# Room by rank of expert resized in a routed mixture of experts, with float32 first layers for seven ranks and wide pairs for two others

## The chip, the cores and the metric

The kernel runs on one core of a Trainium2 chip. The core has five engines that run side by side, each through its own queue in order: TensorE (PE in the profile, its weight loads shown apart as PEld), VectorE (DVE), ScalarE (ACT), GpSimd (POOL) and SyncE (SP), which mainly issues transfers. Transfers run on 16 DMA engines. Matrix products are written to PSUM, a memory of eight banks for each partition; everything else lies in SBUF. The metric is the device time of one execution in microseconds (us).

## The reference, cut to what matters

Two stages follow each other. The first is a recurrent attention with gates over 768 steps for 4 batches and 8 heads; its output, 3072 tokens of 320 numbers, is the input of the second. The change touches the second stage alone:

```python
g_logits = x @ w_group                       # 3072 tokens, 4 groups
g_idx = np.argmax(g_logits, axis=1)          # and its softmax weight g_w
...
e_idx = np.argmax(xg @ w_expert[g], axis=1)  # 4 experts a group, weight e_w
...
h = np.maximum(xg[mask_e] @ w1[g, e], 0.0)   # 320 -> 1024
ye = h @ w2[g, e]                            # 1024 -> 320
out[tok_idx] = (g_w * e_w)[:, None] * ye
```

Each token goes to one of 16 experts, so the number of tokens of an expert is known only on the chip.

## The kernel before, in words

**Routing.** While attention runs, each chunk of 128 steps is routed, and the tokens' numbers are written to a table in device memory (`itab`), a stretch for each expert. The experts are then ranked by their counts, the fullest first. What is compiled is a row of 16 ranks, rank r with fixed room for `CAPS[r]` tokens; which expert stands at a rank is read from a register when its weights are loaded. Rank 0's expert is picked early and done in two pieces, `EARLY` (256) tokens before the routing has ended and `LATE` after it, keys (0, 0) and (0, 1). Tokens beyond the room of their rank are done 128 at a time by a loop at the end (`For_i` at L1062 and what follows), which runs as often as the counts ask.

**An expert.** `load_x` gathers its tokens in blocks of up to 128 rows (GpSimd, L578). `turn_tasks` turns each block with three transposes on TensorE (tile `tpm`) into `xhl`. `expert` then runs a first layer into the tile `psh` (three banks), a Relu into `hh`, and a second layer into `po` (two banks); the rows of `po` are scaled and scattered (L582) to their places in the output.

To keep float32 accuracy at the rate of a single pass, operands are split into a high and a low part (type float32r): `w1h`, `w1l`, `w2h`, `w2l` by `split_tasks` (ScalarE copies, VectorE subtracts, L638 and L640), tokens by `turn_tasks` (L682, L683), and `hh` by `relu` (ScalarE L697, VectorE L700). A first layer has one of three forms:

- Regular (L743): eight matmuls for each of the 8 slices f of 128 hidden units, 64 in all, with the expert's W tokens as moving columns. Two slices share a bank where W is at most 256.
- Wide pairs (`NARROW`, L722 to L728): high and low tokens stand side by side as 2W moving columns; three matmuls of 2W and two of W for each slice, 40 in all, each slice in a bank of its own. ScalarE copies one half out of PSUM and VectorE adds the other, then comes the Relu.
- Float32 (`FULL`, L711): three matmuls of type float32 for each slice, 24 in all, on the unsplit weights `w1s` and unsplit tokens. Nothing of w1 is split for such an expert, and `w1s` stays in use until its first layer ends. The rows of the third part of `xhl` that hold no token are cleared by GpSimd (L677).

The second layer has for each block of tokens 24 matmuls (L764 to L766) with the hidden units as stationary operand and 320 columns of w2 moving. A last block of at most 64 rows (`mp`) takes 16 instead (L769, L770, L772): its high and low hidden units stand side by side in `hh`, as one stationary operand of twice the columns, and the two halves of `po` are added afterwards (L778 to L780).

**Order.** Within the expert stage a scheduler lays out each engine's queue when the kernel is built. `hh` has one buffer; the split weights have two sets, used by ranks of even and odd number; `w1s` and `w2s`, the weights as loaded, have two buffers each. Rank r+2's weights and tokens are asked for at the head of rank r's turn in the loop (SyncE, L596 and L611), but for a `FULL` rank r the load of w1 for rank r+2 is put after r's first layer, since it needs r's buffer. Keys in `RETIRE` let GpSimd wait after their last scatter until its transfers are through (a drain, L786).

Of the kernel before, what the change touches and what calls it, by code (L numbers as in the profile page):

```python
# [7 lines left out]
F32 = mybir.dt.float32  # L8
F32R = mybir.dt.float32r
# [9 lines left out]
P = 128  # L19
# [5 lines left out]
NE = 16  # L25
F = 1024
NF = F // P
# [10 lines left out]

NEARLY, NPICK, EARLY, LATE = 1, 2, 256, 128
CAPS = [EARLY + LATE, 352, 320, 288, 256, 256, 256, 256, 192, 192, 192, 192, 160, 160, 160, 128]


NARROW = ((0, 1), (11, 0), (12, 0))

RETIRE = ((2, 0), (5, 0), (8, 0), (11, 0), (13, 0), (14, 0))


FULL = (13, 14, 15)  # L50


def bc(ap, shape):
# [4 lines left out]
def lstm_moe(ctx: ExitStack, tc: tile.TileContext, gates, qkT, nat, og, wcat, w1, w2, cst, out):  # L58
    nc = tc.nc
    enter = ctx.enter_context  # L60
    mm = nc.tensor.matmul
# [545 lines left out]
    def load_ix(r, q=None):  # L607
        nb = len(blocks(CAPS[r]))
        ixs[r] = mxp.tile([P, 3], I32, name="ix", bufs=5)
# [17 lines left out]
    pools = {}  # L627
# [3 lines left out]
    def split_tasks(r, now=True):  # L631
# [27 lines left out]

        first = [] if r in FULL else [lambda: w1part(0), lambda: w1part(1), wrest]  # L660
        return first + [lambda k=k: w2part(k) for k in range(4)]

    def turn_tasks(key, W, xg, banks=None):
        t = {}

        def one(i, m):
            if i == 0:
                pool = pools["xhl"][len(xhls) % len(pools["xhl"])]
                sh, dt = ([P, 3, W], F32) if key[0] in FULL else ([P, 3, 2, W], F32R)
                t["x"] = xhls[key] = pool.tile(sh, dt, name="xhl", bufs=1)  # L670
# [16 lines left out]
    def expert(key, W, ws, xg, idx, between=(), then=None, last=None):  # L687
        xhl = xhls[key]
        w1h, w1l, wsk, w2h, w2l = (ws.get(n) for n in ("w1h", "w1l", "wsk", "w2h", "w2l"))

        nf = W // P * P if 0 < W % P <= 64 else W
        mp = W - nf
        hh = pools["hp"].tile([P, NF, 2 * W], F32R, name="hh")

        def relu(f, per, src):
            hr = hh[:, f:f + per, 0:W]
            act = nc.scalar.activation(hr, src, AF.Relu)  # L697
            for dst, t in ((slice(W + mp, 2 * W), slice(0, nf)), (slice(W, W + mp), slice(nf, W))):
                if t.start < t.stop:
                    nc.vector.scalar_tensor_tensor(hh[:, f:f + per, dst], src[:, :, t], 0.0, hr.bitcast(F32)[:, :, t],  # L700
                                                   op0=ALU.max, op1=ALU.subtract)
            return act

        if key[0] in FULL:
            w1s = w1st[key[0]]
            for f in range(0, NF, 2):
                ps = pools["ps_h"].tile([P, 512], F32, name="psh")
                for g in range(2):
                    for k in range(3):
                        s = slice(k * F + (f + g) * P, k * F + (f + g + 1) * P)  # L710
                        ins = mm(ps[:, g * W:(g + 1) * W], w1s[:, s], xhl[:, k, :], start=(k == 0), stop=(k == 2))  # L711
                relu(f, 2, ps[:, 0:2 * W].rearrange("p (q w) -> p q w", q=2))
                do(between, 1)
        elif key in NARROW:
            xw, xh = [xhl[:, k].rearrange("p a w -> p (a w)") for k in range(3)], [xhl[:, k, 0, :] for k in range(2)]
            for f in range(0, NF, 2):
                hs = pools["hp"].tile([P, 2, W], F32, name="hs", bufs=2)
                for g in range(2):
                    ps = pools["ps_h"].tile([P, 512], F32, name="psh")
                    s0 = slice((f + g) * P, (f + g + 1) * P)  # L720
                    s1 = slice(F + (f + g) * P, F + (f + g + 1) * P)
                    mm(ps[:, 0:2 * W], w1h[:, s0], xw[0], start=True, stop=False)  # L722
                    mm(ps[:, 0:W], w1l[:, s0], xh[0], start=False, stop=False)
                    mm(ps[:, 0:W], w1l[:, s1], xh[1], start=False, stop=False)
                    mm(ps[:, 0:2 * W], w1h[:, s1], xw[1], start=False, stop=False)
                    ins = mm(ps[:, 0:2 * W], wsk[:, s0], xw[2], start=False, stop=True)
                    nc.scalar.copy(hs[:, g, :], ps[:, W:2 * W])
                    nc.vector.tensor_tensor(hs[:, g, :], hs[:, g, :], ps[:, 0:W], op=ALU.add)  # L728
                act = relu(f, 2, hs)
                if key[0] == 0:  # L730
                    do(between, 1)
        else:
            per = 2 if W <= 256 else 1
            for f in range(0, NF, per):
                ps = pools["ps_h"].tile([P, 512], F32, name="psh")
                for g in range(per):
                    s0 = slice((f + g) * P, (f + g + 1) * P)
                    s1 = slice(F + (f + g) * P, F + (f + g + 1) * P)
                    xh, xl = [xhl[:, k, 0, :] for k in range(3)], [xhl[:, k, 1, :] for k in range(3)]
                    todo = [(w1h, s0, xh[0]), (w1h, s0, xl[0]), (w1h, s1, xh[1]), (w1h, s1, xl[1]), (wsk, s0, xh[2]),  # L740
                            (wsk, s0, xl[2]), (w1l, s0, xh[0]), (w1l, s1, xh[1])]
                    for n, (w, s, x) in enumerate(todo):
                        ins = mm(ps[:, g * W:(g + 1) * W], w[:, s], x, start=(n == 0), stop=(n == len(todo) - 1))  # L743
                relu(f, per, ps[:, 0:per * W].rearrange("p (q w) -> p q w", q=per))
                if per == 2 or f % 2:
                    do(between, 1)
        if then:
            with tc.issue_after(ins.ins):
                do(then)
        if key in NARROW:  # L750
            with tc.issue_after(act.ins):
                do(between)
        for i, m in enumerate(blocks(W)):
            t = slice(i * P, i * P + m)
            tl = slice(W + mp + i * P, W + mp + i * P + m)
            po = pools["ps_o"].tile([P, DM], F32, name="po")
            for f in range(NF):
                s = slice(f * DM, (f + 1) * DM)
                st0, sp0 = f == 0, f == NF - 1
                if last and f == NF // 2 and i == len(blocks(W)) - 1:  # L760
                    with tc.issue_after(ins.ins):
                        do(last)
                if m > 64:
                    mm(po[0:m], hh[:, f, t], w2h[:, s], start=st0, stop=False)  # L764
                    mm(po[0:m], hh[:, f, t], w2l[:, s], start=False, stop=False)  # L765
                    ins = mm(po[0:m], hh[:, f, tl], w2h[:, s], start=False, stop=sp0)  # L766
                else:
                    if not st0:
                        mm(po[0:m], hh[:, f, t], w2l[:, s], start=False, stop=False)  # L769
                    mm(po[0:2 * m], hh[:, f, nf:nf + 2 * m], w2h[:, s], start=st0, stop=sp0)  # L770
                    if st0:
                        mm(po[0:m], hh[:, f, t], w2l[:, s], start=False, stop=False)  # L772
            y = pools["hp"].tile([P, DM], F32, name="y", bufs=3)
            comb = xg[i][0:m, 3 * P:3 * P + 1]
            if m > 64:
                nc.scalar.activation(y[0:m], po[0:m], AF.Copy, scale=comb)  # L776
            else:
                nc.scalar.copy(y[0:m], po[m:2 * m])  # L778
                nc.vector.tensor_tensor(y[0:m], y[0:m], po[0:m], op=ALU.add)
                nc.vector.tensor_scalar(y[0:m], y[0:m], comb, None, op0=ALU.mult)  # L780
            done = scatter(y[0:m], idx(i, m))
            no_order("out", done)
        if key in RETIRE:

            with tc.issue_after(done.ins):
                nc.gpsimd.drain()  # L786
# [241 lines left out]
    for r in range(NEARLY):  # L1028
        xgs[r, 1] = load_x(LATE, late_ix[r])
    xgs[1] = load_x(CAPS[1], ix_of(1))  # L1030
    load_w1(2, nc.gpsimd)
# [4 lines left out]
    with tc.issue_after(rt["last"].ins):  # L1036
        do(split, 3)
    expert((0, 1), LATE, wsp_[0], xgs[0, 1], late_ix[0], split, turn_tasks((1, 0), CAPS[1], xgs[1]))
    xgs[2] = load_x(CAPS[2], ix_of(2))
    for r in range(NEARLY, NE):  # L1040
        if r + 2 < NE:
# [4 lines left out]
            load_w2(r + 2, nc.gpsimd if r < 2 else None)  # L1046
            xgs[r + 2] = load_x(CAPS[r + 2], ix_of(r + 2))
        if r + 1 < NE:
            split = split_tasks(r + 1)
            if r + 1 not in FULL:  # L1050
                do(split, 3)
            then = turn_tasks((r + 1, 0), CAPS[r + 1], xgs[r + 1])
        else:
# [6 lines left out]
    hp = pools["hp"]  # L1060
    nv = nc.values_load(total[0:1, 0:1], min_val=0, max_val=NBLK + NE)
    with tc.For_i(0, nv, 1):  # L1062
# [36 lines left out]
        for f in range(NF):  # L1099
            ps = pools["ps_h"].tile([P, 512], F32, name="psh")  # L1100
            for k in range(3):
                kk = min(P, DM - k * P)
                mm(ps[:, 0:P], w1s[0:kk, k * F + f * P:k * F + (f + 1) * P], xT[0:kk, k, :], start=(k == 0),
                   stop=(k == 2))
            nc.vector.tensor_scalar(h[:, f, :], ps[:, 0:P], 0.0, None, op0=ALU.max)
        po = pools["ps_o"].tile([P, DM], F32, name="po")
        for f in range(NF):
            mm(po, h[:, f, :], w2s[:, f * DM:(f + 1) * DM], start=(f == 0), stop=(f == NF - 1))
        y = hp.tile([P, DM], F32, name="y", bufs=3)
# [69 lines left out]
```

## Time and profile before

| | us |
|---|---|
| median of three runs | 432.39 |
| lowest, highest | 429.99, 433.73 |
| the profiled execution | 433.8 |
| span of the profiled execution, first to last instruction | 432.2 |

The span falls into attention and routing (to about 177 us), rank 0 (to about 205 us), ranks 1 to 15 (to about 426 us) and a tail. Lines of the profile give an engine's busy time, and after a bar what its idle time waited for. A row of a view by stretches gives the stretch, its length, the busy time and number of instructions of TensorE, its weight loads, VectorE, ScalarE and GpSimd, then the granted clock, the share of the DMA engines and GB/s. An instruction counts in a stretch that it overlaps, so a number of instructions can be two or three above those that begin there. A float32 matmul appears as two entries. A row in order of time gives the start, the length, the line, and in brackets how long the engine was idle before it and what released it.

### The profile page before, as it was taken

To read this page: it belongs to the slowest core of one execution; us is meant where nothing else is said; L and a number is where in the kernel's file an instruction comes from. 1 tells how busy PE (TensorE), PEld (TensorE's weight loads), DVE (VectorE), ACT (ScalarE), POOL (GpSimd) and SP (SyncE) were. 2 spreads that over 40 slices of the span, in tenths; PEclk is the share of its full clock that TensorE was granted. 3 is DMA by queue.
4 is the path that set the end of the run, shared out by engine and by line. 5 is a ranking of instruction groups with operands and counts; after the bars stand their busy time and mean duration, and the time that the engine had idled before them with its cause. 6 is when DMAs were issued, how large, how long until landed. Compare 5 with 4: busy or idle time off the path is not lost.

```text
span 432.2 us, 10108 instructions
## 1 busy us (share of the span) xinstructions
PE 406.0 (94%) x3775; PEld 382.5 (89%) x3775; DVE 286.0 (66%) x714; ACT 230.8 (53%) x551; POOL 173.3 (40%) x220
## 2 busy tenths in 40 slices
PE   7879999999998893999999999999999999999994
PEld 4768999898888883799999999999999999999994
DVE  5595677768796963776747585575675877867420
ACT  5654454646566511527637474575656575765421
POOL 2335476666756335154432416213413432322210
PEclk9978899999998987599999999999999999999999
DMA  7974669995999942088975545586559666544300
GB/s 208 286 222 134 191 87 209 264 254 107 248 244 265 224 149 65 3 265 229 424 275 191 200 161 214 170 288 242 211 212 321 211 226 235 186 156 148 153 16 11
DMA packets 29495, 85.39 MB, mean 198 GB/s; under 512 B 12242, under 2 KB 16155, under 8 KB 25861
## 3 DMA queue, kind: packets, MB, share of 16 engines
q1 hardware_dynamic: 24068, 67.63, 54.0%
q0 software_dynamic: 5152, 16.75, 11.2%
q8 instruction: 30, 0.49, 0.5%
q10 hardware_dynamic: 224, 0.35, 0.4%
q14 instruction: 21, 0.16, 0.2%
HBM read 74.95 MB, written 10.62 MB: 198 GB/s over the span
## 4 chain that ended last, share of the span: by engine, by line
PE 71%; issue 11%; DVE 9%; DMA 4%; POOL 2%; POOLq 1%; ACT 1%; DVEq 0%
PE psh L743 21%; PE av L276 6%; PE po L764 6%; PE po L765 6%; PE po L766 6%; PE sp L204 3%; PE it L229 3%; PE tpm L306 3%; DMA sig<-in_og_dram 3%; PE aw L177 2%; PE po L770 2%; PE it L248 2%; PE po L769 2%; PE psh L711 2%; PE tp L306 1%
## 5 line engine op out<-in xcount | busy, mean ns | idle before, releaser
L187 ACT ACTIVATE ab<-aw,bcol 128x128 f32<-128x128 f32 x192 | 54.7, 371 | 53.3 <-PE aw L177 52.9
L578 POOL DMA_INDIRECT xg<-x_d,ix x34 | 40.4, 1189 | 81.5 <-DMA ix<-itab 47.4
L582 POOL DMA_INDIRECT out_dram<-y,ix x34 | 39.8, 1170 | 73.4 <-ACT y L776 58.9
L764 PE MATMUL po<-w2h,hh 128*128 128x320 f32 (+1 forms) x208 | 65.7, 316 | 0.0
L765 PE MATMUL po<-w2l,hh 128*128 128x320 f32 (+1 forms) x208 | 64.2, 309 | 0.0
L766 PE MATMUL po<-w2h,hh 128*128 128x320 f32 (+1 forms) x208 | 64.2, 309 | 0.0
L640 DVE TENSOR_TENSOR w2l<-w2s,w2h 128x640 fp32r<-128x640 f32 x64 | 50.2, 818 | 20.1 <-ACT w2h L638 20.1
L743 PE MATMUL psh<-xhl,w1h 128*128 128x256 f32 (+4 forms) x352 | 59.5, 290 | 0.9 <-DVE xhl L683 0.5
L276 PE MATMUL av<-nt,pt 128*128 128x128 f32 x384 | 52.9, 295 | 0.2 <-DVE pt L209 0.2
L743 PEld LDWEIGHTS psh<-xhl,w1h 128*128 128x128 f32 x352 | 50.3, 192 | 1.5 <-DVE xhl L683 0.8
L276 PEld LDWEIGHTS av<-nt,pt 128*128 128x128 f32 x384 | 50.4, 210 | 1.0 <-DVE pt L209 0.4
L700 DVE SCALAR_TENSOR_TENSOR hh<-psh,hh 128x256 fp32r<-128x256 f32 (+2 forms) x104 | 39.6, 413 | 15.4 <-ACT hh L697 14.9
L697 ACT ACTIVATE hh<-psh 128x512 fp32r<-128x512 f32 (+5 forms) x68 | 33.4, 491 | 30.6 <-PE psh L743 21.9
L638 ACT CAST w2h<-w2s 128x640 fp32r<-128x640 f32 x64 | 43.1, 725 | 0.2 <-DMA w2s<-in_w_dram 0.2
L640 DVE TENSOR_TENSOR w1l<-w1s,w1h 128x1024 fp32r<-128x1024 f32 x26 | 31.7, 1221 | 11.1 <-ACT w1h L638 8.8
L764 PEld LDWEIGHTS po<-w2h,hh 128*128 128x128 f32 (+1 forms) x208 | 38.9, 187 | 0.1
L765 PEld LDWEIGHTS po<-w2l,hh 128*128 128x128 f32 (+1 forms) x208 | 38.9, 187 | 0.0
L766 PEld LDWEIGHTS po<-w2h,hh 128*128 128x128 f32 (+1 forms) x208 | 38.8, 187 | 0.0
L209 DVE TENSOR_TENSOR pt<-sp,ab 128x512 f32<-128x512 f32 x48 | 31.1, 686 | 11.2 <-PE sp L204 9.6
L776 ACT ACTIVATE y<-po,xg 128x320 f32<-128x320 f32 (+1 forms) x26 | 13.7, 528 | 45.4 <-PE po L766 40.2
L743 PE MATMUL psh<-xhl,wsk 128*128 128x256 f32 (+4 forms) x176 | 36.5, 289 | 0.0
L743 PE MATMUL psh<-xhl,w1l 128*128 128x256 f32 (+4 forms) x176 | 36.3, 288 | 0.0
(192 smaller groups left out, 824.6 us busy)
## 6 DMA issues: line engine op xcount, KB each, us to landing
w1s<-in_w_dram SPq DMA_DIRECT2D x12, 1536.0 KB, 7.0
w2s<-in_w_dram SPq DMA_DIRECT2D x12, 1280.0 KB, 6.9
qk<-in_qkT_dram SPq DMA_DIRECT2D x48, 192.0 KB, 7.1
nt<-in_nat_dram SPq DMA_DIRECT2D x24, 324.0 KB, 6.8
x_d<-x SPq DMA_DIRECT2D x24, 192.0 KB, 6.8
sig<-in_og_dram SPq DMA_DIRECT2D x6, 640.0 KB, 6.8
w1s<-in_w_dram SPq DMA_DIRECT2D x4, 768.0 KB, 12.1
w1s<-in_w_dram POOLq DMA_DIRECT2D x2, 1536.0 KB, 8.5
```

What stands on the lines that cost most here:

```text
L187: rt["exp"] = nc.scalar.activation(st_[u]["ab"][:, r, j, :], aw[:, j, :], AF.Exp, bias=bcol[:, c, i:i + 1])
L276: ins = mm(av[:, i:i + P], t["pm"][r][:, pr, :], nt[:, o:o + P], start=True, stop=True)
L578: return nc.gpsimd.indirect_dma_start(out=o, out_offset=None, in_=src, in_offset=bass.IndirectOffsetOnAxis(ap=idx, axis=0))
L582: return nc.gpsimd.indirect_dma_start(out=out, out_offset=bass.IndirectOffsetOnAxis(ap=idx, axis=0), in_=y, in_offset=None, bounds_check=N ...
L638: nc.scalar.copy(a, src[:, s])
L640: lows.append(lambda: nc.vector.tensor_tensor(o[rows], src[rows, s], a[rows].bitcast(F32), op=ALU.subtract))
L697: act = nc.scalar.activation(hr, src, AF.Relu)
L700: nc.vector.scalar_tensor_tensor(hh[:, f:f + per, dst], src[:, :, t], 0.0, hr.bitcast(F32)[:, :, t], op0=ALU.max, op1=ALU.subtract)
L743: ins = mm(ps[:, g * W:(g + 1) * W], w[:, s], x, start=(n == 0), stop=(n == len(todo) - 1))
L764: mm(po[0:m], hh[:, f, t], w2h[:, s], start=st0, stop=False)
L765: mm(po[0:m], hh[:, f, t], w2l[:, s], start=False, stop=False)
L766: ins = mm(po[0:m], hh[:, f, tl], w2h[:, s], start=False, stop=sp0)
```

## The change

The room by rank becomes smaller nearly everywhere. By rank, before and after (rank 0 is `EARLY` + `LATE`):

| rank | 0 | 1 | 2 | 3 | 4 | 5 | 6 | 7 | 8 | 9 | 10 | 11 | 12 | 13 | 14 | 15 |
|---|---|---|---|---|---|---|---|---|---|---|---|---|---|---|---|---|
| before | 256+128 | 352 | 320 | 288 | 256 | 256 | 256 | 256 | 192 | 192 | 192 | 192 | 160 | 160 | 160 | 128 |
| after | 256+80 | 304 | 288 | 272 | 256 | 240 | 224 | 208 | 176 | 160 | 144 | 144 | 144 | 128 | 128 | 96 |

The sum goes from 3744 to 3248. Wide pairs were used for (0, 1) and ranks 11 and 12, and are now used for (0, 1) and ranks 7 and 8. Float32 first layers were those of ranks 13 to 15, and are now those of ranks 9 to 15.

A last block may now have 48 or 16 rows, where it had 64 or 32. A half of `po` that is read by itself begins at partition 32 or 64, so the low part of such a block begins at column `mo` = 32 or 64 of the side-by-side operand, and the `mo - mp` columns between are cleared by GpSimd once for each such expert. The diff, whole but for its context:

```diff
-NEARLY, NPICK, EARLY, LATE = 1, 2, 256, 128
-CAPS = [EARLY + LATE, 352, 320, 288, 256, 256, 256, 256, 192, 192, 192, 192, 160, 160, 160, 128]
+NEARLY, NPICK, EARLY, LATE = 1, 2, 256, 80
+CAPS = [EARLY + LATE, 304, 288, 272, 256, 240, 224, 208, 176, 160, 144, 144, 144, 128, 128, 96]
-NARROW = ((0, 1), (11, 0), (12, 0))
+NARROW = ((0, 1), (7, 0), (8, 0))
-FULL = (13, 14, 15)
+FULL = tuple(range(9, NE))
...
         mp = W - nf
-        hh = pools["hp"].tile([P, NF, 2 * W], F32R, name="hh")
+        mo = mp if mp == 0 else 32 if mp <= 32 else 64
+        wl = nf + mo + mp
+        hh = pools["hp"].tile([P, NF, nf + wl], F32R, name="hh")
+        if mo > mp:
+            nc.gpsimd.memset(hh[:, :, W:nf + mo].bitcast(F32), 0.0)
...
-            for dst, t in ((slice(W + mp, 2 * W), slice(0, nf)), (slice(W, W + mp), slice(nf, W))):
+            for dst, t in ((slice(wl, wl + nf), slice(0, nf)), (slice(nf + mo, wl), slice(nf, W))):
...
-            tl = slice(W + mp + i * P, W + mp + i * P + m)
+            tl = slice(wl + i * P, wl + i * P + m)
...
-                    mm(po[0:2 * m], hh[:, f, nf:nf + 2 * m], w2h[:, s], start=st0, stop=sp0)
+                    mm(po[0:mo + m], hh[:, f, nf:wl], w2h[:, s], start=st0, stop=sp0)
...
-                nc.scalar.copy(y[0:m], po[m:2 * m])
+                nc.scalar.copy(y[0:m], po[mo:mo + m])
```

Here `nf` counts the rows in full blocks (a remainder over 64 rows counts as full), `mp` those of a small last block.

## The prediction

> **What bounds the kernel now.** I read the page first, for the busiest engine and the chain that ended last.
>
> ```profile
> span 432.2 us, 10108 instructions
> PE 406.0 (94%) x3775; PEld 382.5 (89%) x3775; DVE 286.0 (66%) x714; ACT 230.8 (53%) x551; POOL 173.3 (40%) x220
> PE 71%; issue 11%; DVE 9%; DMA 4%; POOL 2%; POOLq 1%; ACT 1%; DVEq 0%
> ```
>
> TensorE carries the chain, but 94% is a mean over two halves. So I cut the span into stretches: attention, the experts from rank 1 on, first layers alone (from an expert's first psh matmul to the first turn after it, found in the order of time of TensorE), turns, second layers, tail.
>
> ```profile
> core 0: us, PE busy (x) PEld busy (x) DVE busy (x) ACT busy (x) POOL busy (x), PEclk, DMA share, GB/s
> 194.63:199.71 5.08, 5.02 (x43) 4.73 (x42) 2.27 (x9) 3.18 (x11) 3.16 (x4) 1.00 0.77 260
> 203.77:214.86 11.09, 11.09 (x72) 11.07 (x71) 8.89 (x14) 7.06 (x14) 4.87 (x4) 1.00 0.99 416
> 226.13:235.67 9.54, 9.54 (x67) 9.39 (x66) 6.52 (x18) 6.16 (x13) 2.48 (x2) 1.00 0.47 153
> 246.04:254.61 8.57, 8.57 (x67) 8.56 (x66) 7.07 (x20) 5.94 (x13) 2.33 (x3) 1.00 0.44 154
> 264.64:272.12 7.48, 7.48 (x67) 7.48 (x65) 5.68 (x9) 4.99 (x9) 3.67 (x2) 1.00 0.60 213
> 325.41:332.54 7.13, 7.13 (x67) 7.13 (x66) 4.72 (x10) 4.65 (x9) 2.54 (x3) 1.00 0.95 350
> 339.06:346.26 7.20, 7.20 (x67) 7.20 (x66) 5.62 (x12) 4.67 (x9) 3.84 (x4) 1.00 0.99 325
> 352.77:359.93 7.16, 7.16 (x67) 7.16 (x66) 5.59 (x12) 4.66 (x9) 5.80 (x4) 1.00 0.92 325
> 359.93:360.50 0.57, 0.57 (x8) 0.57 (x7) 0.00 (x0) 0.57 (x1) 0.00 (x0) 1.00 0.93 341
> 366.46:372.99 6.53, 6.49 (x43) 5.83 (x41) 3.84 (x13) 3.77 (x11) 3.87 (x4) 1.00 0.89 307
> 379.50:385.39 5.89, 5.80 (x43) 5.31 (x42) 3.52 (x13) 3.46 (x11) 0.91 (x1) 1.00 0.64 238
> 391.89:398.41 6.52, 6.52 (x51) 6.52 (x50) 5.35 (x12) 4.12 (x8) 1.95 (x1) 1.00 0.60 214
> 411.45:411.70 0.25, 0.25 (x5) 0.25 (x4) 0.00 (x0) 0.04 (x1) 0.00 (x0) 1.00 0.00 0
> 417.63:422.90 5.27, 5.27 (x50) 5.27 (x49) 2.12 (x5) 1.57 (x4) 0.88 (x1) 1.00 0.10 34
> 422.90:426.43 3.53, 3.53 (x27) 3.51 (x25) 0.42 (x1) 0.39 (x1) 0.00 (x0) 1.00 0.00 0
> 426.43:432.20 5.77, 0.24 (x2) 0.00 (x0) 0.00 (x0) 0.53 (x1) 0.98 (x1) 0.87 0.05 18
> 205.00:426.50 221.50, 221.37 (x1645) 217.89 (x1643) 139.71 (x262) 126.66 (x240) 70.85 (x61) 1.00 0.58 207
> ```
>
> The row for 205.00 to 426.50 decides: TensorE works for 221.37 of 221.50 us, at full granted clock, while VectorE has 139.71 and ScalarE 126.66. From rank 1 to the tail the time is the sum of TensorE's instructions. What the change takes off there comes off the end, as long as no other engine or transfer takes TensorE's place.
>
> The other rows are a price list, in order: (0, 1) with 128 tokens as wide pairs; rank 1 with 352; ranks 2, 3 and 4 with 320, 288 and 256; ranks 8, 9 and 10 with 192; a two-block turn; ranks 11 and 12, wide pairs of 192 and 160; rank 13, float32 with 160; a one-block turn; rank 15, float32 with 128; its second layer; the tail. Rank 1 is partly interleaved with the block before it, so its rate comes from the chain of waits:
>
> ```profile
> 205.01 9.86 PE psh L743 x61
> ```
>
> Per matmul: 9.86/61 = 0.1616 us at 352 columns, 9.54/64 = 0.1491 at 320, 8.57/64 = 0.1339 at 288, 7.48/64 = 0.1169 at 256, 7.16/64 = 0.112 at 192. Down to 256 the time follows the columns, 0.47 ns for each between 352 and 256; from 256 to 192 it falls by 0.08 ns for each: a floor of about 0.11. Float32 takes 48 entries an expert, two for each of 24 matmuls: 6.52/48 = 0.1358 at 160 and 5.27/48 = 0.1098 at 128. A second-layer matmul of 320 columns takes 3.53/24 = 0.147.
>
> **The change part by part.** First layers, priced between their neighbours. Rank 1, 352 to 304: midway between 0.1339 and 0.1491 is 0.1415, times 64 is 9.06, against 64 x 0.1616 = 10.34: -1.28. Rank 2, 320 to 288: 8.57 for 9.54, -0.97. Rank 3, 288 to 272: midway between 8.57 and 7.48, -0.54. Rank 4 stays. Ranks 5 and 6, 256 to 240 and 224, lie between 7.48 and 7.16: -0.08 and -0.16 on the line, -0.32 each if the floor already holds; I take the line, the nearer rows.
>
> Ranks 7 and 8 become wide pairs (40 matmuls for 64, and a copy on ScalarE and an addition on VectorE for each f). The pairs of 384 and 320 columns took 6.53 and 5.89 with their small stalls on that copy and addition included: 0.01 us for each column. So 416 columns give 6.85 for 7.48, -0.63, and 352 give 6.21 for 7.13, -0.92. Bounds: by their columns alone, 8 x 1664 and 8 x 1408 at 0.1616/352 us, they would take 6.11 and 5.17, 0.74 and 1.04 less; or stalls as much longer. In rank 7 nothing of w1 is split for rank 9 any more, so VectorE has no more to do there than in rank 11 now.
>
> Ranks 9 to 12 become float32. Rank 9, 160 tokens: 6.52 for 7.20, -0.68. With 144 tokens, midway between 5.27 and 6.52, a first layer is 5.90: rank 10 -1.26 (from 7.16), rank 11 -0.63 (from 6.53), rank 12 +0.01 (from 5.89). Ranks 13 and 14, 160 to 128: 6.52 to 5.27, -1.25 each. Rank 15, 128 to 96: between 5.27 (the floor) and 96/128 of it, 3.96; I take 5.27, since 192 columns in a single pass stood at the floor too, and keep -1.31 for the range.
>
> [...] No row here shows a float32 first layer under 128 columns. [...]
>
> Rank 0's late block, wide pairs of 128 to 80 tokens: 24 of its 40 matmuls go from 256 columns to the floor, 24 x (0.1169 - 0.11) = -0.17, and the other 16 stood there already (0, or all 40 at the floor without a stall: 4.4 for 5.08, -0.68).
>
> Second layers: 24 matmuls for each full block, 16 for a remainder of up to 64. Rank 1's third block falls from 96 to 48 rows: 8 fewer, 8 x 0.147 = -1.18. Ranks 13 and 14 lose their block of 32: 16 fewer each, -2.35 each. Elsewhere the blocks keep their kind; a stationary operand of 80 or 112 columns for 128 still streams 320. A turn of two blocks (0.57) becomes one (0.25) ahead of ranks 13 and 14: -0.32 each.
>
> Sum: 0.17 + 1.28 + 1.18 + 0.97 + 0.54 + 0.08 + 0.16 + 0.63 + 0.92 + 0.68 + 1.26 + 0.63 - 0.01 + 2 x (1.25 + 2.35 + 0.32) = 16.3 us.
>
> Off TensorE. The splits of w1 for ranks 9 to 12 go, from ScalarE and VectorE; I count nothing, since both stand a third idle under TensorE. Two gathers and two scatters go from GpSimd, also nothing. What comes new needs its cover named. (a) In six experts (ranks 1, 3, 8, 10, 11, 12) GpSimd clears the gap in hh between the remainder's two parts. hh has one buffer, so the clearing waits for the second layer before, but only the remainder's matmuls read it, ten or more us later: 0, if only they wait. (b) Seven experts clear part of xhl (L677) instead of three, 0.2 us each, an expert ahead: 0. (c) w1 of ranks 11 to 15 is loaded only when the first layer two ranks before has released its buffer, and what stands behind it in SyncE's queue waits too.
>
> ```profile
> w1s<-in_w_dram SPq DMA_DIRECT2D x12, 1536.0 KB, 7.0
> w2s<-in_w_dram POOLq DMA_DIRECT2D x2, 1280.0 KB, 16.5
> xg<-x_d,ix POOLq DMA_INDIRECT x34, 4.9
> ix<-itab SPq DMA_DIRECT2D x11, 1.0 KB, 5.5
> ```
>
> From the end of rank r's first layer to the start of rank r+2's lie r's turn and second layer and all of r+1. For rank 11's weights that is 0.57 + 5.96 + 5.90 + 6.5 = 18.9 us, for rank 15's, the shortest, 0.25 + 3.53 + 5.27 + 0.25 + 3.53 = 12.8. A load takes 7.0, so it is in time; the indices behind it (5.5) and the gather (4.9) have two experts' time as well: 0.
>
> The profiled execution took 433.8 us around its span of 432.2; less 16.3 it would be 417.5. It stands 1.4 above the median of the runs, 432.39, from which I forecast 416.1.
>
> **The rivals.**
>
> First, GpSimd's clearing of hh holds the expert up. If the first Relu into hh waits for it too, TensorE runs on only until its three psh banks are full.
>
> ```profile
> 210.69 0.95 POOL L578 DMA_INDIRECT xg<-x_d,ix  x1 [0.30 <-issue]
> 247.90 1.28 POOL L582 DMA_INDIRECT out_dram<-y,ix  x1 [0.88 <-DVE y L780]
> 337.52 1.77 POOL L578 DMA_INDIRECT xg<-x_d,ix  x1 [8.96 <-PE po L766]
> 342.67 1.14 POOL L582 DMA_INDIRECT out_dram<-y,ix  x1 [0.30 <-issue]
> 393.70 1.95 POOL L582 DMA_INDIRECT out_dram<-y,ix  x1 [2.07 <-DVE y L780]
> L786 POOLq DRAIN  x6: 2312/5146/7983, 247.7 to 419.2; - x6
> L677 POOL MEMSET xhl<- x3: 200/231/256, 373.3 to 398.7; 64x160 f32 x2, 64x128 f32 x1
> ```
>
> Around a change of expert GpSimd works through gathers and scatters in order: rank 9 began at 339.06 and the queue was through at 343.81, 4.75 later; at rank 1, begun at 205.01, it was through at 211.64, 6.6 later; at rank 3, begun at 246.04, at 249.18, 3.1 later, and then a drain (L786) of 5.1 at the median; at rank 13, begun at 391.89, at 395.65, 3.8 later, and rank 12 looks the same with a drain before it. Three banks cover 3 x 12 x 0.123 = 4.4 in float32, 3 x 8 x 0.1415 = 3.4 at rank 1, 3.0 at rank 3, 2.3 in wide pairs. Queued last, the clearing costs 0.3 each at ranks 10 and 11, 2.4 at rank 8, 3.2 at rank 1, 5.2 at rank 3, 4.5 at rank 12: 15.9, which gives 432.0; with the longest drain (7.98) twice, 438, slower than before. It decides from drains just over the median. For it: one buffer, an engine in order, drains ahead of ranks 3 and 12. Against it: no byte is shared between the clearing and any Relu, and where the clearing comes ahead of the scatters it costs nothing. Half of that price would give 424.
>
> Second, w1 comes late in the float32 experts. A load at 16.5, as when four were queued at once near 200 us, would be 3.7 late at rank 15 and 1.3 at rank 14 (lead 15.2): 421. Against it: one load of 1.5 MB and one of 1.3 in 9 to 12 us, where the stretch of rank 1's first layer moved 416 GB/s.
>
> Third, the room is too small for the drawn tokens and the loop over what is left runs, which has not one row in this trace. The reference's own routing gives 321, 290, 274, 257, 242, 239, 209, 193, 165, 158, 139, 135, 132, 126, 125, 67 tokens by rank; each fits, rank 5 with 1 to spare (239 of 240). One turn of the loop, from rows: indices 5.5, weights 7.0 to 16.5, a first layer of 5.27, a second of 16 float32 entries of 320 columns at twice 0.1358, 4.3: 22 to 32 us, so 438 to 448.
>
> [...]
>
> **How the numbers follow.** The forecast, with all its small bounds, 0.75. The clearing at half its price or less, 0.07 (418 to 425), nearer to all of it, 0.07 (426 to 438). Late weights, 0.07 (417 to 425). The loop, 0.03. Columns for little, 0.01. The range: below, the floor does not hold at rank 15 (1.31), ranks 5 and 6 at the floor (0.40), rank 0's late block (0.51) and wide pairs by their columns alone (1.78) together give 412.1, so 412.0; above, up to the clearing's half price, 424.0. A measurement of this kernel tells about 1% from no change. Faster by more: 0.75 + 0.07 + 0.07 + 0.01, 0.90; within 1%, 0.05; slower, 0.05.
>
> **What would show each step.** The float32 line goes from 144 entries to 336, the first layers' regular line from 704 to 448, the second layers from 768 matmuls to 728. First layers of 9.06, 8.57, 8.03, 6.85, 6.21, 6.52 and 5.90 us for ranks 1, 2, 3, 7, 8, 9 and 10; ranks 13 and 14 in 9.05 from start to start. TensorE without a gap from rank 1 to a tail that still takes 5.8 (426.43 to 432.20). Wrong: idle TensorE early in ranks 1, 3, 8 or 12 with a clearing just ended on GpSimd; a wait on w1s ahead of float32 matmuls; rows of the loop; rank 15 at 4.0 in its first layer.

## The result and the profile after

| | before | after |
|---|---|---|
| median of the first comparison (four runs each), us | 432.26 | 414.85 |
| lowest, highest | 429.99, 433.73 | 413.5, 416.81 |
| median of a second comparison (11 and 6 runs) | 431.98 | 417.02 |
| the profiled execution | 433.8 | 414.25 |
| its span | 432.2 | 412.6 |

The ratio is 0.9605 with an interval of 0.9546 to 0.9664 in the first comparison, and 0.9656 (0.9606 to 0.9706) in the second. All ten runs of the changed kernel together have a median of 416.2; 416.1 was forecast.

First the page of the changed kernel: span, engines, and the chain that ended last by engine.

```profile
span 412.6 us, 9857 instructions
PE 386.7 (94%) x3665; PEld 361.5 (88%) x3665; DVE 262.6 (64%) x692; ACT 213.7 (52%) x541; POOL 167.8 (41%) x226
PE 70%; DMA 12%; issue 9%; POOL 3%; DVE 3%; POOLq 1%; ACT 1%; SPq 0%; DVEq 0%
```

TensorE lost 19.3 us of work, the span 19.6, and the share stayed 94%: the bound is the same engine. That is the sign of a change that removed work from the bound and put no wait in its place. The same stretches as before show where, again from the first `psh` matmul of an expert to its next turn: rank 0's late block, ranks 1, 2, 3, 4, 5, 6, 7, 8, 9 and 10, then ranks 13 and 14 whole (to the next expert's start), rank 15, the tail, and all from rank 1 on.

```profile
core 0: us, PE busy (x) PEld busy (x) DVE busy (x) ACT busy (x) POOL busy (x), PEclk, DMA share, GB/s
192.16:196.61 4.45, 4.45 (x42) 4.45 (x41) 1.92 (x9) 2.71 (x11) 2.83 (x3) 1.00 0.78 251
201.12:210.14 9.02, 9.02 (x66) 8.97 (x65) 8.08 (x20) 6.01 (x13) 4.25 (x4) 1.00 1.00 415
220.45:229.01 8.56, 8.56 (x66) 8.52 (x65) 7.05 (x20) 5.92 (x13) 3.28 (x3) 1.00 0.56 188
239.38:247.58 8.20, 8.20 (x67) 8.09 (x65) 6.92 (x20) 5.79 (x13) 2.41 (x3) 1.00 0.39 149
257.56:265.16 7.60, 7.60 (x67) 7.60 (x66) 5.68 (x9) 4.99 (x9) 3.65 (x2) 1.00 0.65 227
272.86:280.04 7.18, 7.18 (x66) 7.18 (x65) 4.83 (x7) 4.88 (x9) 2.53 (x3) 1.00 0.97 350
287.68:294.82 7.14, 7.14 (x66) 7.14 (x65) 4.72 (x7) 4.80 (x9) 1.64 (x2) 1.00 0.92 331
302.54:309.27 6.73, 6.73 (x42) 6.08 (x41) 3.10 (x9) 4.03 (x11) 2.92 (x3) 1.00 0.79 309
316.94:323.17 6.23, 6.18 (x43) 5.60 (x42) 2.92 (x11) 3.72 (x11) 1.64 (x3) 1.00 0.53 201
329.68:336.19 6.51, 6.51 (x50) 6.51 (x49) 5.35 (x12) 4.13 (x8) 1.97 (x1) 1.00 0.61 228
342.71:348.58 5.87, 5.87 (x50) 5.87 (x49) 5.08 (x12) 4.04 (x8) 3.27 (x4) 1.00 0.79 305
379.54:388.74 9.20, 9.20 (x78) 9.20 (x77) 5.30 (x10) 4.82 (x11) 3.21 (x3) 1.00 0.78 264
388.74:397.95 9.21, 9.21 (x77) 9.21 (x76) 4.45 (x8) 4.73 (x11) 1.02 (x1) 1.00 0.22 91
397.95:403.23 5.28, 5.28 (x51) 5.28 (x49) 1.07 (x3) 1.52 (x4) 0.99 (x1) 1.00 0.10 33
406.90:412.60 5.70, 0.07 (x1) 0.00 (x0) 0.00 (x0) 0.52 (x1) 0.92 (x1) 0.95 0.06 18
201.12:406.80 205.68, 205.63 (x1539) 200.52 (x1537) 117.98 (x240) 110.53 (x230) 63.18 (x66) 1.00 0.62 223
```

The last row answers to the row of 221.50 us that decided the prediction: again TensorE works in all of it but 0.05 us. How much of the 19.6 us is the change's own? The part that it touches runs from the late block's first `psh` matmul to the last second-layer matmul. Before it ran from 194.63 to 426.51, 231.9 us; after from 192.16 to 406.81, 214.7 us: 17.2 less. The other 2.5 us lie ahead of it, in attention, routing and rank 0's first 256 tokens, which the change does not reach. The late block's start wanders from execution to execution, whatever the rooms: 195.92 in the kernel below with all the new rooms, 192.66 in the one with all the old.

The groups of instructions of the changed kernel show that the float32 form and the regular form run as often as foreseen:

```profile
L715 PE MATMUL psh<-xhl,w1s 128*128 128x144 f32 (+3 forms) x336 | 41.3, 283 | 0.0
L747 PE MATMUL psh<-xhl,w1h 128*128 128x256 f32 (+5 forms) x224 | 38.6, 295 | 0.9 <-DVE xhl L683 0.5 <-ACT xhl L682 0.4
```

All of L747 is 448 matmuls (224 on w1h, 112 each on w1l and wsk), the second layers' lines together 728. The body of the loop over what is left has no row.

GpSimd in order of time shows the clearing of `hh` (L697) at ranks 1 and 3, whose first layers began at 201.12 and 239.38, with what stands around it:

```profile
200.87 1.70 POOL L578 DMA_INDIRECT xg<-x_d,ix  x1 [0.30 <-DVE xhl L683]
202.55 0.24 POOL L697 MEMSET hh<- 128x128 f32 x1
202.97 0.96 POOL L582 DMA_INDIRECT out_dram<-y,li  x1 [0.18 <-issue]
239.42 0.97 POOL L578 DMA_INDIRECT xg<-x_d,ix  x1 [0.30 <-PE po L773]
240.38 0.22 POOL L697 MEMSET hh<- 128x128 f32 x1
241.19 1.22 POOL L582 DMA_INDIRECT out_dram<-y,ix  x1 [0.58 <-DVE y L784]
```

It stands behind one gather and ahead of the scatter, so it ends within 1.7 us of an expert's start. At ranks 8, 10, 11 and 12 it begins 0.3 us after the start.

### The profile page after: what moved, and what is told of

It reads as the page before. It is cut to its first block, busy times and chain, and to the rows that moved or that the text cites. A ratio compares the mean times of both kernels' runs of the same rounds, so it can differ in the third digit from the quotient of the medians.

```text
span 412.6 us, 9857 instructions
## 1 busy us (share of the span) xinstructions
PE 386.7 (94%) x3665; PEld 361.5 (88%) x3665; DVE 262.6 (64%) x692; ACT 213.7 (52%) x541; POOL 167.8 (41%) x226
## 4 chain that ended last, share of the span: by engine, by line
PE 70%; DMA 12%; issue 9%; POOL 3%; DVE 3%; POOLq 1%; ACT 1%; SPq 0%; DVEq 0%
PE psh L747 14%; PE av L276 7%; PE po L769 6%; PE po L768 6%; PE po L770 6%; PE psh L715 6%; PE sp L204 4%; DMA w2s<-in_w_dram 3%; PE it L229 3%; PE tpm L306 3%; PE aw L177 2%; DMA itab<-tokid,slot 2%; PE it L248 2%; DMA nt<-in_nat_dram 2%; PE po L774 2%
## 5 line engine op out<-in xcount | busy, mean ns | idle before, releaser
L768 PE MATMUL po<-w2h,hh 128*128 128x320 f32 (+3 forms) x200 | 63.1, 316 | 0.0
L770 PE MATMUL po<-w2h,hh 128*128 128x320 f32 (+3 forms) x200 | 61.8, 309 | 0.0
L769 PE MATMUL po<-w2l,hh 128*128 128x320 f32 (+3 forms) x200 | 61.8, 309 | 0.0
L704 DVE SCALAR_TENSOR_TENSOR hh<-psh,hh 128x256 fp32r<-128x256 f32 (+4 forms) x108 | 36.0, 366 | 18.0 <-ACT hh L701 17.5
L701 ACT ACTIVATE hh<-psh 128x288 fp32r<-128x288 f32 (+8 forms) x68 | 30.1, 443 | 30.1 <-PE psh L747 15.4
L638 ACT CAST w2h<-w2s 128x640 fp32r<-128x640 f32 x64 | 43.2, 724 | 0.4 <-DMA w2s<-in_w_dram 0.4
L715 PE MATMUL psh<-xhl,w1s 128*128 128x144 f32 (+3 forms) x336 | 41.3, 283 | 0.0
L715 PEld LDWEIGHTS psh<-xhl,w1s 128*128 128x128 f32 x336 | 40.9, 191 | 0.1
L747 PE MATMUL psh<-xhl,w1h 128*128 128x256 f32 (+5 forms) x224 | 38.6, 295 | 0.9 <-DVE xhl L683 0.5
L209 DVE TENSOR_TENSOR pt<-sp,ab 128x512 f32<-128x512 f32 x48 | 31.0, 685 | 10.2 <-PE sp L204 9.3
L769 PEld LDWEIGHTS po<-w2l,hh 128*128 128x128 f32 (+3 forms) x200 | 36.5, 183 | 0.0
L768 PEld LDWEIGHTS po<-w2h,hh 128*128 128x128 f32 (+3 forms) x200 | 36.5, 182 | 0.0
L770 PEld LDWEIGHTS po<-w2h,hh 128*128 128x128 f32 (+3 forms) x200 | 36.4, 182 | 0.0
L747 PEld LDWEIGHTS psh<-xhl,w1h 128*128 128x128 f32 x224 | 32.5, 196 | 1.5 <-DVE xhl L683 0.8
L204 PE MATMUL sp<-qk 40*128 40x128 f32 x384 | 29.5, 286 | 1.3 <-DVE pt L209 1.3
```

Source lines behind the costliest of these rows:

```text
L204: mm(t["pm"][r][:, pr, :], qk[rs, 0, pr, :], qk[rs, 1, pr, :], start=True, stop=True)
L638: nc.scalar.copy(a, src[:, s])
```

## The experiments

All edits are to the changed kernel. Ratios are to the kernel before, run beside each. "Rank 1 to the end" is the time from rank 1's first `psh` matmul to the last second-layer matmul, 205.7 us in the changed kernel; it leaves out the wandering of attention.

**The new rooms with the old forms.** The theory: the rooms give most of it, and the forms the last 2 to 3 us.

```diff
-NARROW = ((0, 1), (7, 0), (8, 0))
+NARROW = ((0, 1), (11, 0), (12, 0))
-FULL = tuple(range(9, NE))
+FULL = (13, 14, 15)
```

> The new rooms with the forms of before (wide pairs for (0, 1), ranks 11 and 12, float32 for ranks 13 to 15). Theory, TensorE's sum: against the changed kernel rank 7 goes back to regular (7.14 for 6.73 us in its first layer, the floor), rank 8 (7.13 for 6.23), ranks 9 and 10 (7.13 for 6.52 and for 5.88), and ranks 11 and 12 become wide pairs of 288 columns (about 5.6 for 5.88 each): +0.41 + 0.90 + 0.61 + 1.25 - 0.28 - 0.28 = +2.6, so 417.5 where the changed kernel has 414.9. Rival, the forms are what pays (four experts without a split of w1): half of the 17 us or more goes, 423 or more. Rival, the forms are worth nothing: 415.

Measured: 419.85 us, ratio 0.9705 (0.9658 to 0.9751); rank 1 to the end 208.8, 3.1 more than with the new forms. The stretches are the first layers of ranks 8, 10 and 12.

```profile
321.13:328.24 7.11, 7.11 (x66) 7.11 (x65) 4.61 (x10) 4.56 (x9) 2.58 (x4) 1.00 0.96 343
348.48:355.58 7.10, 7.10 (x66) 7.10 (x65) 5.17 (x12) 4.41 (x9) 6.18 (x4) 1.00 0.82 300
374.58:380.21 5.63, 5.51 (x42) 5.09 (x41) 3.34 (x13) 3.25 (x11) 1.07 (x2) 1.00 0.63 242
```

176 and 144 columns both take 7.1 us for 64 matmuls, 0.111 each, and 240 and 224 took 7.18 and 7.14 above: in the regular form a smaller room buys next to nothing below 240 columns. Only a form with fewer matmuls does, as the last row, a wide pair of 288 columns, shows.

**The old rooms with the new forms.** `CAPS`, `LATE` and the code for `hh` as before, `NARROW` and `FULL` as changed.

```diff
-CAPS = [EARLY + LATE, 304, 288, 272, 256, 240, 224, 208, 176, 160, 144, 144, 144, 128, 128, 96]
+CAPS = [EARLY + LATE, 352, 320, 288, 256, 256, 256, 256, 192, 192, 192, 192, 160, 160, 160, 128]
```

> The rooms of before with the new forms (wide pairs for (0, 1), ranks 7 and 8, float32 for ranks 9 to 15). Theory, TensorE's sum: rank 7 as pairs of 512 columns about as before (7.5 to 7.9 for 7.49), rank 8 as pairs of 384 6.53 for 7.13, ranks 9, 10 and 11 as float32 of 192 columns 6.52 x 192/160 = 7.82 for 7.20, 7.16 and 6.53, rank 12 as float32 of 160 6.52 for 5.89: +0.2 - 0.60 + 0.62 + 0.66 + 1.29 + 0.63 = +2.8, so slower than before, about 435. Rival, the forms pay by themselves through fewer splits: 432 or less.

Measured: 434.92 us, ratio 1.0087 (1.0052 to 1.0122). First layers of ranks 7 (pairs of 512 columns) and 9 (float32 with 192 tokens):

```profile
308.24:315.84 7.60, 7.60 (x43) 6.29 (x42) 3.98 (x9) 4.56 (x11) 2.40 (x3) 1.00 0.70 272
336.59:344.39 7.80, 7.80 (x51) 7.78 (x50) 5.57 (x12) 4.40 (x8) 1.99 (x1) 1.00 0.59 197
```

At the old rooms these two cost more than the regular form (7.52 and 7.19). Rank 8 as wide pairs gains (6.54 for 7.13); most of the loss is that of ranks 11 and 12, float32 in place of wide pairs (7.80 for 6.53 and 6.52 for 5.89). So the two halves of the change do not add: the forms alone lose 3.0 us by the medians (434.92 for 431.95) and 2.6 from rank 1 to the end, on the new rooms they gain 3.1.

**The clearing, made to be waited for.** Theory: it comes in time whatever waits for it. Rival: if a Relu waits for it, TensorE stands. Here the clearing takes in the last column that the Relu itself writes, so that each Relu of that expert must wait for it.

```diff
-            nc.gpsimd.memset(hh[:, :, W:nf + mo].bitcast(F32), 0.0)
+            nc.gpsimd.memset(hh[:, :, W - 1:nf + mo].bitcast(F32), 0.0)
```

> The changed kernel, but GpSimd's clearing of the gap in hh begins one column earlier, on a column that every Relu writes afterwards, so each Relu into hh has to wait for the clearing in the six experts that have one. Theory: the clearing stands ahead of the scatters and within 1.3 us of the expert's start, less than three psh banks cover: 415, within 1 us of the changed kernel. Rival of the prediction: the clearing stands behind gathers, scatters and a drain in GpSimd's queue, and the wait costs up to 15.9 us: 418 to 431.

Measured: 416.39 us, ratio 0.9654 (0.961 to 0.9698); rank 1 to the end 205.8, 0.1 more. Where it stands in GpSimd's queue, even a needless wait costs nothing.

**The clearing late, with and without that column.** To price the rival, the clearing is put behind the last scatter and drain of the expert before it. In the first kernel it shares the column with the Relu, in the second it does not.

```diff
+            with tc.issue_after(rt["pool"].ins):
-            nc.gpsimd.memset(hh[:, :, W:nf + mo].bitcast(F32), 0.0)
+                nc.gpsimd.memset(hh[:, :, W - 1:nf + mo].bitcast(F32), 0.0)
...
+        rt["pool"] = done
...
-                nc.gpsimd.drain()
+                rt["pool"] = nc.gpsimd.drain()
```

> The changed kernel with the rival of the prediction made true: GpSimd's clearing of hh is put behind the last scatter of the rank before (and its drain, where it has one), and begins one column earlier, so that every Relu waits for it. By the prediction's way of pricing (when GpSimd is through, less what three psh banks cover) with the changed kernel's own rows: rank 1 1.4 us, rank 3 5.0, rank 8 none, rank 10 1.9, rank 11 0.2, rank 12 5.7, together 14, so 429 (425 to 433). Rival: VectorE and ScalarE catch up and the wait is absorbed: 415 to 418.

> The same late place of the clearing, but on the gap alone, with no column that a Relu writes. Theory: only the remainder's matmuls wait for it, long after, so 415 to 416, as the changed kernel. Rival: the clearing's wait holds up GpSimd's gathers and scatters behind it, or the Relu waits for the tile as a whole: 418 or more.

Measured, with two executions of each: with the shared column 442.19 us, ratio 1.0202 (1.0168 to 1.0237), 13 us above what was expected; without it 416.11, ratio 0.96 (0.9543 to 0.9657). Of the first kernel: GpSimd in order of time around the change to rank 3 (begun at 241.87), ScalarE's group of Relus, and stretches with the granted clock in the column behind GpSimd's busy time.

```profile
243.68 3.43 POOL L582 DMA_INDIRECT out_dram<-y,ix  x1 [0.81 <-DVE y L785]
254.48 0.22 POOL L698 MEMSET hh<- 128x136 f32 x1 [7.37 <-issue]
```
```profile
L702 ACT ACTIVATE hh<-psh 128x288 fp32r<-128x288 f32 (+8 forms) x68 | 29.3, 444 | 56.9 <-POOL hh L698 21.4 <-PE psh L748 17.9 <-PE psh L716 17.1
```
```profile
241.87:255.18 13.31, 3.15 (x26) 2.93 (x24) 3.81 (x7) 3.37 (x7) 4.65 (x4) 0.76 0.51 186
255.18:257.00 1.82, 1.82 (x7) 1.82 (x8) 1.31 (x6) 0.53 (x2) 0.95 (x1) 0.50 0.14 21
201.90:435.15 233.25, 214.91 (x1538) 208.44 (x1537) 118.19 (x240) 110.68 (x230) 69.74 (x65) 0.95 0.54 193
```

GpSimd stood 7.4 us between scatter and clearing, where the drain is; the clearing came 12.6 us after rank 3's first matmul, and TensorE worked 3.15 of 13.31 us. The last row splits the price: TensorE stood 18.3 us (233.25 - 214.91), and its work took 214.91 instead of 205.63, 9.3 us more, with the granted clock down, as behind rank 3's stand to 0.50, and to 0.95 in the mean. Of these 9.3 us 1.6 are rank 1's, where the clock fell before the clearing came, behind another stand (1.83 us, until 200.51), which is explained below; 7.7 are left to the clearing. The rival's mechanism is real. It needs a shared byte and a late place at once, and the changed kernel has neither.

**Ranks 13 and 14 with their old room.** To measure the largest term by itself.

```diff
-CAPS = [EARLY + LATE, 304, 288, 272, 256, 240, 224, 208, 176, 160, 144, 144, 144, 128, 128, 96]
+CAPS = [EARLY + LATE, 304, 288, 272, 256, 240, 224, 208, 176, 160, 144, 144, 144, 160, 160, 96]
```

> The changed kernel with rooms of 160 again for ranks 13 and 14: the largest term of the sum undone. Theory: each gets 1.25 us more in the float32 first layer, 16 second-layer matmuls (2.35) and a second turned block (0.32): 2 x 3.92 = +7.8, so 422.7. Rival: the tail and the transfers hide part of it, since little is loaded by then: 419 or less.

Measured: 423.28 us, ratio 0.978 (0.9737 to 0.9823). The two experts whole, as stretches:

```profile
381.54:394.57 13.03, 13.03 (x97) 12.63 (x96) 5.90 (x14) 5.70 (x14) 4.67 (x6) 1.00 0.74 275
394.57:407.28 12.71, 12.71 (x93) 12.31 (x92) 5.90 (x14) 5.42 (x12) 2.94 (x2) 1.00 0.04 14
```

25.74 us against 18.41, and the turn ahead of them 0.57 against 0.24: 7.7 us, for 7.84 predicted. (Rank 1 to the end took 9.0 us more; the other 1.4 are rank 1's, and are explained below.) More than half of it is the last block's 16 second-layer matmuls, which go only where the room comes down to a whole 128.

**Wide pairs further down.** At 160 columns a wide pair first layer should take 5.9 us by the price list (float32: 6.51), and at 144 some 5.6 (5.87). If so, pairs in ranks 9 to 12 beat float32.

```diff
-NARROW = ((0, 1), (7, 0), (8, 0))
+NARROW = ((0, 1), *((r, 0) for r in range(7, 13)))
-FULL = tuple(range(9, NE))
+FULL = (13, 14, 15)
```

> The changed kernel with wide pairs for ranks 9 to 12 in place of float32 (float32 for ranks 13 to 15 only). Theory, TensorE's sum: rank 9 as pairs of 320 columns 5.89 for 6.52, ranks 10, 11 and 12 as pairs of 288 columns about 5.6 for 5.88: -0.63 - 3 x 0.28 = -1.5, so 413.4, a little faster than the changed kernel. Rival: w1 of four more experts has to be split (3.2 us of ScalarE and 3.7 us of VectorE for each), beside the pairs' own copies and additions; TensorE waits for its psh banks and it comes out at 415 or more.

A miss: 417.48 us, ratio 0.9667 (0.9623 to 0.9712); rank 1 to the end 209.1, 3.4 more. Stretches: the first layers of ranks 9, 10 and 12; then VectorE at the head of rank 9 and TensorE's stall there, in order of time.

```profile
329.63:337.01 7.38, 5.83 (x42) 5.31 (x41) 5.88 (x16) 3.89 (x12) 1.93 (x2) 1.00 0.75 253
343.80:350.64 6.84, 5.52 (x42) 5.05 (x41) 5.42 (x16) 3.55 (x12) 2.43 (x4) 1.00 0.79 251
370.70:376.32 5.62, 5.50 (x42) 5.07 (x41) 3.33 (x13) 3.24 (x11) 1.06 (x2) 1.00 0.63 240
```
```profile
331.32 1.22 DVE L640 TENSOR_TENSOR wsk<-w1s,wsk 64x1024 fp32r<-64x1024 f32 x1
...
332.88 0.77 DVE L732 TENSOR_TENSOR hs<-hs,psh 128x160 f32<-128x160 f32 x3
```
```profile
333.24 0.41 PE L726 MATMUL psh<-xhl,w1h 128*128 128x320 f32 x1 [1.46 <-DVE hs L732]
```

TensorE's own work was as cheap as thought (5.83 and 5.52 us), but the first layers of ranks 9, 10 and 11 stood 1.3 to 1.6 us for VectorE's addition, which each wide pair needs before its bank is free and which was queued behind a split of w1 for the next rank. Rank 12, in whose time nothing of w1 is split, took the 5.62 expected. Float32 is the better form there not by its matmuls but because it needs neither the addition nor the split. The four first layers together make 2.5 of the 3.4 us; the rest lies in the second layers of ranks 7 to 10; why is open.

**Pairs only where no split should fall: ranks 9 and 12.**

```diff
-NARROW = ((0, 1), (7, 0), (8, 0))
+NARROW = ((0, 1), (7, 0), (8, 0), (9, 0), (12, 0))
-FULL = tuple(range(9, NE))
+FULL = (10, 11, 13, 14, 15)
```

> Wide pairs only where no split of w1 falls into the pairs' first layer: ranks 7, 8, 9 and 12 as pairs, ranks 10, 11 and 13 to 15 float32. Theory from the run with pairs up to rank 12: a stall on VectorE's additions comes where three splits of w1 are still in its queue; without them rank 9 takes about 5.9 for 6.52 us and rank 12 5.62 for 5.88, so 0.9 less, minus 0.2 of second layers: from r1 on 0.7 us shorter than the changed kernel, 414.2, which the runs' spread can hardly tell from 414.9; the first layers in the trace tell it. Rival: rank 9 still stalls, 7 us or more in its first layer.

Measured: 417.72 us, ratio 0.9658 (0.9607 to 0.9709); rank 1 to the end 206.3, 0.6 more where 0.7 less was expected: a miss. Rank 9 took 5.92 and rank 12 5.62, as expected, but rank 11 took 13.54 us whole instead of 12.37: rank 12's w1 has to be split in rank 11's time and landed late, and its splits stood ahead of the work on `hh`. ScalarE, in order of time:

```profile
355.26 1.05 ACT L638 CAST w1h<-w1s 128x1024 fp32r<-128x1024 f32 x1 [1.47 <-DMA w1s<-in_w_dram]
```

**The changed kernel again, and a wait that was found beside the experiments.** In the traces of several of these kernels TensorE stood at the end of rank 0's late block. Is that theirs, or also the changed kernel's?

> The changed kernel again, on the same chip as the two runs beside it, and a second trace of it. Theory: the expert stage from rank 1's first matmul to the last one takes 205.7 us as in the first trace, within 0.3; what moves between executions lies ahead of it, in attention and routing, and at the start of rank 1. 415, within 2.

The expectation of 205.7 was missed: 207.1, all of it at rank 1's start; from rank 2 on the stages agree with the first trace to 0.02 us. TensorE in order of time, and stretches across it (the stand, three stretches of 3.41 us each, rank 1's first layer):

```profile
200.13 0.37 PE L768 MATMUL po<-w2h,hh 128*80 128x320 f32 x1 [1.90 <-ACT hh L701]
```
```profile
198.20:200.13 1.93, 0.03 (x2) 0.00 (x1) 1.93 (x5) 1.93 (x6) 1.44 (x2) 1.00 0.85 281
198.28:201.69 3.41, 1.56 (x10) 1.42 (x11) 3.41 (x7) 3.08 (x7) 1.57 (x3) 1.00 0.92 346
201.69:205.10 3.41, 3.41 (x16) 3.41 (x15) 3.32 (x6) 2.48 (x6) 2.49 (x2) 0.50 0.99 419
205.10:208.51 3.41, 3.41 (x26) 3.41 (x25) 2.36 (x8) 1.81 (x5) 0.05 (x1) 1.00 1.01 422
201.15:211.62 10.47, 10.47 (x67) 10.47 (x65) 8.31 (x20) 6.22 (x13) 2.75 (x3) 0.84 1.00 406
```

The last Relu of the late block stands in ScalarE's queue behind the first cast of rank 2's w1 (L638). In the kernel before it stood there too, began 16.6 us after its transfer was asked for (by GpSimd), and held nobody. In the changed kernel the cast began at 196.71 in the first trace, right behind the copy ahead of it, so that it waited for nothing, 16.7 us after its transfer was asked for at 180.00. In this one ScalarE was free for it at 195.60, but it began at 196.78, 18.9 us after its transfer was asked for at 177.84. Here everything ahead had ended early: TensorE began the late block at 189.99 instead of 192.16, came to the place before the cast was done, and stood. The other traces with the new rooms go the same way: in all seven in which the late block began before 191.4 TensorE stood, there or, with the cast moved, one stage later; in the four in which it began at 191.7 or later it did not. Then came a second price: about 1.6 us after it went on, the granted clock fell to 0.50 for 3.4 us (201.69 to 205.10), and rank 1's first layer took 10.47 for 9.02. So this execution was 2.2 us ahead at the late block and 1.5 us behind at the end of rank 1's first layer, and from the late block to the end it took 218.3 us: 13.6 less than before, not 17.2.

**The cast moved behind that Relu, alone and with rank 9 as pairs.**

```diff
-                act = relu(f, 2, hs)
+                act = rt["act"] = relu(f, 2, hs)
...
-            if r + 1 not in FULL:
+            if r == 1:
+                with tc.issue_after(rt["act"].ins):
+                    do(split, 3)
+            elif r + 1 not in FULL:
```

> The changed kernel, with the copies that split rank 2's w1 put behind the last Relu of rank 0's late block in ScalarE's queue. Theory: where routing ends early, these weights land some 18 us after their issue and the copy ahead of that Relu holds it, so that TensorE waits about 2 us in the late block's second layer (in the traces of the runs with blocks back, with pairs for 9 and 12 and with the clearing held); with the copy behind, no trace shows that wait, and the time is 0 to 2 us less than that of the changed kernel on the same chip. Rival: rank 2's weights are then split too late, or the wait comes back at rank 1's first layer: the same time or up to 2 us more.

> As the run before, and wide pairs for rank 9 too, float32 from rank 10 on. Theory: rank 9's first layer takes 5.9 us for 6.5, since no split of w1 is made for ranks 10 and 11, less 0.2 in a second layer: 0.4 us less than the run before. Rival: the split of rank 9's w1, now among rank 7's pairs, stalls them: rank 7's first layer over 7 us, and nothing is won.

Measured: 416.11 us, ratio 0.9617 (0.9566 to 0.9669), and with the pairs 416.8, ratio 0.964 (0.9595 to 0.9685). The late block's second layer was back at 3.61 us (5.80 with the wait), but the stand came back one stage later, in rank 1's first layer. Of the kernel with the cast moved alone, TensorE in order of time and a stretch behind it:

```profile
204.78 1.10 PE L747 MATMUL psh<-xhl,w1h 128*128 128x304 f32 x4 [1.81 <-DVE hh L704]
```
```profile
206.00:208.00 2.00, 2.00 (x10) 2.00 (x10) 1.61 (x6) 0.42 (x1) 0.00 (x0) 0.50 1.06 442
```

Rank 1's first layer ended at 211.98, against 211.62 without the move, in an execution whose late block had begun 0.5 later: nothing gained. The 0.6 us of rank 9 (5.94 for 6.52) is there in the trace of the second kernel, less 0.2 in rank 7's second layer; 0.4 us is too little for these medians. No version tried is measurably faster than the changed kernel.

## Why the prediction was right, point by point

**The bound.** TensorE alone, by the sum of its instructions. Right: 16.3 us were forecast, and from the late block to the end 17.2 were measured in the first trace and 13.6 in the second, where the wait just shown gave 3.6 back. Against the medians the change gave 17.4 and 15.0 us. The terms below, as the first trace has them, add to 16.9; the other 0.3 lies in stages that were counted at nothing. That the median of all ten executions, 416.2, lies so near the forecast of 416.1 is partly luck: in the first trace the sum was 0.9 us too small, and in the second a wait that it left out took 3.6 us.

**First layers by columns.** Rank 1: 9.02 for 9.06. Rank 2: 8.56 for 8.57. Rank 3: 8.20 for 8.03; the saving, 0.37, is two thirds of its term, so the line between 256 and 288 columns is not straight. Rank 4, which keeps its 256 columns, took 7.60 us, where the four ranks with 256 columns took 7.47 to 7.52 before; why is open. Ranks 5 and 6 stood at the floor already: 7.18 and 7.14, 0.3 less each, where I took 0.08 and 0.16 off the line and kept the floor as a bound. "Columns for little", at 0.01 in the forecast, is out: no run shows it above 256 columns, where from 288 to 304 a matmul went from 0.1338 to 0.1409 us, 0.45 ns a column.

**Wide pairs.** Rank 7: 6.73 for 6.85. Rank 8: 6.23 for 6.21. Rank 0's late block was mis-sized, the largest error of all terms: 4.45 for 4.91, so 0.63 us saved and not 0.17. All its 40 matmuls are at the floor (4.45/40 = 0.111 us each) and the stall on the addition is gone, which was the bound of 4.4.

**Float32.** Rank 9: 6.51 for 6.52. Rank 10: 5.87 for 5.90, and ranks 11 and 12 the same. Rank 15 with 96 columns: 5.28 for 5.27, 0.110 us an entry, as at 128, where 144 columns took 5.87/48 = 0.122. That is the floor.

**Blocks.** Rank 1's second layer: 10.52 us with the old room and 9.41 with the new, 1.11 for 1.18. Ranks 13 and 14: 9.20 and 9.21 us from start to start for 9.05, since a first layer took 5.35 and not 5.27 and a second 3.60 and not 3.53; 7.7 of 7.84.

**The clearing counted at nothing.** Right, by both reasons that the prediction held against the rival. It argued from the bytes, that no Relu shares one, and allowed that an early place would do as well. The run with the late place and no shared byte shows that the first alone is enough; the run with the shared byte and the early place shows that the place alone is enough too. My price for the rival, 15.9 us, came near the 18.3 that TensorE stood in the kernel built to suffer it, but by luck: rank 3 stood 10.2 for 5.2, ranks 10 and 11 2.7 and 1.9 for 0.3 each, rank 12 3.3 for 4.5, and ranks 1 and 8 0.1 each for 3.2 and 2.4. What it lacked was the clock, 7.7 us more.

**Late weights.** No float32 expert waited: rank 15's w1 was asked for at 385.08, needed at 397.95, and such loads took 6.9 us at the median. What the step did not list is rank 2's w1, whose cast held the late block up in one of the two traces of the changed kernel. I priced that block by its columns and did not ask what TensorE would reach sooner. It costs 1.9 us and 1.5 more by the clock, and it is why an early end of routing earned nothing in the second trace. What the cast itself waits for until 196.8 stays open: the profile names a transpose that was long done, and no landing of that transfer is recorded in the traces with the stand. In the first trace the two transfers of w1 that GpSimd asked for landed 6.6 and 7.7 us later.

**The loop.** It never ran. That holds for the tokens drawn here, of which rank 5 has 239 in 240 places; another draw could overflow a room, and no run here shows that price.

## What to carry to other kernels

Where one engine works without a gap, price a change by a list of what its instructions took at neighbouring sizes, and look in that list for steps: here a block of rows (7.7 us for two) and the number of matmuls counted for more than columns, and below 240 columns a regular first layer got hardly any cheaper (7.18 us at 240, 7.10 at 144). A form that is cheaper on the bound can lose through the other engines' queues, as the wide pairs did behind the splits of w1 (stands of 1.3 to 1.6 us); and a form and a size have to be judged together, since the same forms lost about 3 us at the old rooms and gained 3 at the new. When an engine gets to a place sooner, ask which transfer or cast it will now meet there.

## What the runs showed of the hardware that was not expected

A short stand can cost more than its length, and whether it does hangs on when it falls. In six traces TensorE stood 1.8 to 1.9 us near rank 1's start. In five of them (the changed kernel again, ranks 13 and 14 with their old room, the late clearing with the shared column, and both with the cast moved) the granted clock fell to 0.50 for 3.4 us, 0.3 to 1.6 us after TensorE went on. Rank 1's first layer then ran at a mean granted clock of 0.84 to 0.88, and its matmuls took 1.4 to 1.8 us more. In the sixth, with pairs in ranks 9 and 12, the same place stood 1.80 us and the clock stayed at 1.00, with rank 1's first layer at 9.07; a stand of 1.10 us (the late clearing without the shared column) left it at 1.00 too. Of the sixth trace, TensorE in order of time, a stretch of 3.41 us and the stretch of that layer:

```profile
200.72 0.37 PE L768 MATMUL po<-w2h,hh 128*80 128x320 f32 x1 [1.80 <-ACT hh L701]
```
```profile
199.01:202.43 3.42, 1.71 (x11) 1.56 (x12) 3.39 (x8) 3.09 (x7) 1.44 (x3) 1.00 0.90 349
201.74:210.81 9.07, 9.07 (x67) 8.96 (x66) 8.12 (x20) 6.02 (x13) 2.75 (x3) 1.00 1.02 418
```

The traces themselves show what tells the sixth from the others. In each of the thirteen every change of the granted clock lies on a grid of 3.41 us: in the changed kernel again the clock came back at 177.80, fell at 201.69, seven steps later, and came back at 205.10, one step later. From 190 us on, in all thirteen, a step of the grid was followed by a clock of 0.50 wherever TensorE had stood 1.81 us or more of it, and by 1.00 wherever it had stood 1.71 or less. In the five traces at least 1.81 us of the stand lay in one step, as in 198.28 to 201.69 above. In the sixth an edge at 199.01 cut the stand, which ran from 198.92 to 200.72, so that 1.71 us of it lay in the step that followed, and 0.09 in the one before.

The bound between 1.71 and 1.81 us is that of the expert stage alone: in attention the clock also fell behind steps in which TensorE had stood less, 0.61 us of the step from 41.63 in the kernel before. What sets the grid, and why the clock falls behind such a step, no run here shows.
